# Batch 0's hidden layer by seven products of quarters with sums kept in SBUF, and weight sums and fold in one buffer each

## Chip, cores and metric

The kernel runs on one core of a Trainium2 chip. The metric is device time in microseconds (us), the median of five executions. One further execution was recorded by the hardware profiler; its records are the profile and the trace spoken of below. Engines are named as there: PE (TensorE matmul), PEld (its weight load), DVE (VectorE), ACT (ScalarE), POOL (GpSimd), SP (SyncE, which issues most DMAs).

## What is computed

Four batches of 768 rows pass through attention with hash buckets and then through a Fourier mixing layer with a two-layer channel network:

```python
mask = q_bucket[:, :, :, None] == k_bucket[:, :, None, :]
scores = np.where(mask, scale * (q @ k.T), -1e9)          # (4, 8, 768, 768)
attn = softmax(scores);  x = attn @ v                     # x: (4, 768, 512)
mixed = np.real(fft(fft(x, axis=1), axis=2))
u = x + mixed
un = (u - mean(u)) / sqrt(var(u) + 1e-6)
out = u + np.maximum(un @ w_ch1, 0.0) @ w_ch2             # w_ch1: 512 x 2048, w_ch2: 2048 x 512
```

`w_ch1` and `w_ch2` arrive in 64-bit form, and the kernel narrows them to 32 bits itself. All large products are float32.

## The kernel before

**Stages.** Batch b's attention (`attention`, L912) goes over four pairs of heads, and for each over six tiles of 128 keys, so it has 24 steps. A step computes scores for both heads (`weigh`, L837: PE L856, exponentials on ACT L860, the bucket mask on DVE L866), adds the weights up over key tiles in `acc` (DVE L944) and multiplies the weights of the step before by v (`values`, L872: PE L877). Weights lie in two buffers, `pk`, used in turn. After the sixth tile `scale` (L882) turns the sums into reciprocals (PE L897, DVE L901 to L910) and scales x.

Mixing of batch b (`mix`, L1017) is a generator which is advanced between the attention steps of batch b+1; `MIX`, its number of steps less `LEFT` = 8, is spread over the 24 steps (22 for batch 1). So two streams of work share each engine's queue, and a scheduler fixes the final order of every queue when the kernel is built. `mix` has these parts: `fold` (L984, DVE) forms even and odd parts of x in `ef` and writes `z`; L1034 and L1063 (PE) are the Fourier products, whose results ACT (L1041, L1047) and DVE (L1077) take up; then comes the channel network.

**Hidden layer, two ways.** Batches 1 to 3 use `mlp7` (L1314). It treats `un @ w_ch1` as a product of 2 x 2 quarters and needs seven products where the plain way needs eight. For each of 8 row blocks f, PE computes seven products (L1348: two 128x384 matmuls each) into banks `p1`, `p6`, `p5`, `p7`. They come from a pool of two PSUM buffers; two of the seven accumulate on an earlier product's bank. ACT copies the banks out (L1370, L1373, L1380, L1385, L1389, L1397), DVE adds the copies (L1374, L1381, L1386, L1390, L1398), and ACT applies ReLU (L1377, L1387, L1391, L1399). Three sums of quarters of x (`t1`, `t2`, `t4`, DVE L1334 to L1336, and `t3` in place, L1341) are its right operands. Its left operands, quarters of `w_ch1` and four sums of them, come back from DRAM (`ad`) through a ring of 12 buffers in `w1`'s space.

Batch 0 uses `mlp0` (L1282): eight products per row block straight from `w1` (L1301), and per bank one ReLU on ACT (L1305), nothing on DVE. While it runs, `quarters(f)` (L1129) forms the four sums of row block f on DVE (L1136 to L1139) in `tq` and SP writes them and three plain quarters to `ad` for the later batches; `quarters` for the next f waits until `tq` has been written out.

**Outer layer.** `outer7` (L1194) multiplies half of the hidden rows by `w_ch2`, also by seven products (L1219), so the order in a batch is: first four row blocks, `outer7`, last four row blocks, `outer7`.

**Second weight.** During batch 0's mixing `weights2` (L1161) narrows 16 slices of `w_ch2`. Each is fetched by a DMA on POOL's queue (L677) into one of three raw buffers `zraw2`, then worked on by DVE (L631, L635, L644, and the sums L1185 to L1188) and ACT (L639, L646, L647). The raw buffer is fetched into again when L644 and L647 are through. The first eight slices must be there before the first `outer7`, the last eight can be written only after it and must be there before the second.

**Buffers.** `acc` and `ef` share a pair of buffers, tag `t6`, used in turn.

## Time and profile before

| | |
|---|---|
| Five executions | 1111.12, 1114.02, 1115.25, 1116.39, 1118.21 us; median 1115.25 |
| Profiled execution | 1116.28 us, of which the span of the trace is 1114.5 us |
| PE busy | 1070.0 us, 96% of the span |
| DVE busy | 779.0 us, 70% |
| ACT busy | 453.8 us, 41% |
| POOL busy | 79.7 us, 7% |
| Mean granted PE clock | 0.992 |
| Batch 0's direct products, L1301 | 256 recorded matmuls, from 200.5 us to 381.0 us |
| Seven-product row blocks of batches 1 to 3, L1348 | 672 recorded matmuls |
| Raw slices of `w_ch2`, L677 | 512 KB each, median 4.9 us from issue to landing |

A 32-bit matmul is recorded as two instructions: 128 matmuls of the program are the 256 of L1301. A group's busy time is the time in which at least one of its instructions runs, and[...] a stream of 384-column matmuls of 493 ns each can start every 320 ns or so.

### The profile page before, as it was taken

To read this page: it belongs to the slowest core of one execution; us is meant where nothing else is said; L and a number is where in the kernel's file an instruction comes from. 1 tells how busy PE (TensorE), PEld (TensorE's weight loads), DVE (VectorE), ACT (ScalarE), POOL (GpSimd) and SP (SyncE) were. 2 spreads that over 40 slices of the span, in tenths; PEclk is the share of its full clock that TensorE was granted. 3 is DMA by queue.
4 is the path that set the end of the run, shared out by engine and by line. 5 is a ranking of instruction groups with operands and counts; after the bars stand their busy time and mean duration, and the time that the engine had idled before them with its cause. 6 is when DMAs were issued, how large, how long until landed. Compare 5 with 4: busy or idle time off the path is not lost.

```text
span 1114.5 us, 13886 instructions
## 1 busy us (share of the span) xinstructions
PE 1070.0 (96%) x4917; PEld 654.7 (59%) x4917; DVE 779.0 (70%) x1298; ACT 453.8 (41%) x875; POOL 79.7 (7%) x141
## 2 busy tenths in 40 slices
PE   6989997999999999999999999999999999999996
PEld 3434353555755576655664567645674568768675
DVE  5779977737699595985767796884766875644353
ACT  5767455535054224354325522354315422341420
POOL 0000000001200011030000011021000002100000
PEclk9999999999999999999999999999999999999998
DMA  9743535521037144223144235122032215122401
GB/s 230 191 99 86 109 106 164 156 88 35 1 105 231 42 91 156 43 62 83 32 142 94 72 63 169 26 51 91 24 98 82 71 34 170 46 88 70 139 19 41
DMA packets 175566, 103.13 MB, mean 93 GB/s; under 512 B 129408, under 2 KB 162816, under 8 KB 175488
## 3 DMA queue, kind: packets, MB, share of 16 engines
q1 hardware_dynamic: 168400, 83.93, 28.3%
q0 software_dynamic: 5520, 17.83, 5.1%
q8 instruction: 41, 0.67, 0.2%
q10 hardware_dynamic: 1568, 0.39, 0.2%
q14 instruction: 37, 0.30, 0.1%
HBM read 81.14 MB, written 20.97 MB: 92 GB/s over the span
## 4 chain that ended last, share of the span: by engine, by line
PE 63%; DVE 14%; ACT 2%; issue 2%; DMA 1%; DVEq 0%; ACTq 0%
PE o L1219 23%; PE h_p L1348 18%; PE oo L877 5%; PE h L1301 5%; PE sc L856 5%; DVE pk L866 4%; DVE acc L944 2%; PE cs L1034 2%; PE A L1063 1%; DMA zraw<-in_moe_w_ch_dram 1%; PE B L1063 1%; DVE x L1077 1%; ACT pk L860 1%; PE bits L791 1%; PE sum L897 1%
## 5 line engine op out<-in xcount | busy, mean ns | idle before, releaser
L1219 PE MATMUL o<-w,h 128*128 128x256 f32 x1152 | 258.9, 381 | 0.1
L1219 PEld LDWEIGHTS o<-w,h 128*128 128x128 f32 x1152 | 216.6, 190 | 42.7 <-issue 4.7
L860 ACT ACTIVATE pk<-sc 128x768 f32<-128x768 f32 x192 | 148.2, 808 | 100.9 <-PE sc L856 72.0
L866 DVE SCALAR_TENSOR_TENSOR pk<-qb,kb,pk 128x768 f32<-128x768 bf16 x132 | 128.5, 1012 | 63.3 <-ACT pk L860 62.7
L877 PE MATMUL oo<-pk,vn 128*64 128x385 f32 (+1 forms) x768 | 152.5, 505 | 4.5 <-ACT x L890 3.0
L856 PE MATMUL sc<-qt,kt 64*128 64x384 f32 x768 | 153.7, 505 | 1.9 <-ACT pk L860 1.9
L1348 PE MATMUL h_p<-x,w 128*128 128x384 f32 x384 | 139.0, 493 | 1.4 <-ACT h L1389 1.4
L944 DVE TENSOR_TENSOR acc<-acc,pk 128x1536 f32<-128x1536 f32 (+1 forms) x72 | 105.6, 1480 | 2.4 <-ACT pk L860 1.9
L1348 PE MATMUL h_p<-w 128*128 128x384 f32 x288 | 106.0, 491 | 0.7 <-ACT u L1090 0.7
L877 PEld LDWEIGHTS oo<-pk,vn 128*64 128x64 f32 x768 | 48.9, 137 | 96.0 <-issue 76.1
L1348 PEld LDWEIGHTS h_p<-x,w 128*128 128x128 f32 x384 | 70.4, 190 | 57.7 <-ACT h L1389 5.1
L856 PEld LDWEIGHTS sc<-qt,kt 64*128 64x128 f32 x768 | 66.4, 186 | 48.8 <-issue 24.9
L1301 PE MATMUL h<-x,w 128*128 128x384 f32 x256 | 86.5, 492 | 1.8 <-ACT h L1305 1.8
L1348 PEld LDWEIGHTS h_p<-w 128*128 128x128 f32 x288 | 53.3, 190 | 41.0 <-ACT w L1397 3.3
L1301 PEld LDWEIGHTS h<-x,w 128*128 128x128 f32 x256 | 47.5, 190 | 38.4 <-ACT h L1305 3.0
L1249 ACT COPY tq<-o 128x256 f32<-128x256 f32 x24 | 8.9, 372 | 115.5 <-PE o L1219 115.5
L1231 DVE SCALAR_TENSOR_TENSOR w<-o,rs,w 128x256 f32<-128x256 f32 x56 | 26.7, 478 | 40.7 <-PE o L1219 40.7
L1219 PE MATMUL o<-w 128*128 128x256 f32 x192 | 46.1, 383 | 3.9 <-DVE w L1231 2.4
L972 POOL DMA_DIRECT2D out_dram<-w x30 | 16.3, 546 | 428.3 <-issue 309.0
L1219 PEld LDWEIGHTS o<-w 128*128 128x128 f32 x192 | 35.9, 190 | 11.4 <-DVE w L1231 4.5
L1238 ACT COPY tq<-o 128x256 f32<-128x256 f32 x24 | 8.9, 371 | 74.8 <-PE o L1219 74.8
L1265 DVE TENSOR_TENSOR tq<-tq,o 128x256 f32<-128x256 f32 x24 | 10.1, 421 | 38.1 <-PE o L1219 38.1
(158 smaller groups left out, 1272.8 us busy)
## 6 DMA issues: line engine op xcount, KB each, us to landing
w<-ad SPq DMA_DIRECT2D x168, 128.0 KB, 2.0
w<-bd SPq DMA_DIRECT2D x42, 512.0 KB, 4.5
zraw<-in_moe_w_ch_dram POOLq DMA_DIRECT2D x21, 512.0 KB, 4.9
bd<-w SPq DMA_DIRECT2D x14, 512.0 KB, 5.0
vn<-in_v_dram SPq DMA_DIRECT2D x32, 192.0 KB, 3.5
qn<-in_q_dram SPq DMA_DIRECT2D x120, 48.0 KB, 2.4
kn<-in_k_dram SPq DMA_DIRECT2D x60, 96.0 KB, 3.4
ad<-tq SPq DMA_DIRECT2D x8, 512.0 KB, 3.3
```

What stands on the lines that cost most here:

```text
L856: last[0] = nc.tensor.matmul(ps[:, h, 0:HALF], kt[rows, ks], qt[rows, qs], start=kb is not None, stop=True,)
L860: nc.scalar.activation(pk[:, g, :, 0:HALF], ps[:, :, 0:HALF], AF.Exp, scale=SCALE)
L866: nc.vector.scalar_tensor_tensor(w, qb[:, h].rearrange("p (g s) -> p g s", g=2), kb[:, h, c : c + 1], w, op0=ALU.is_equal, op1=ALU.mult,)
L877: nc.tensor.matmul(oos[g][h * D : (h + 1) * D, 0:w], nat["v", n][:, (2 * c + h) * D : (2 * c + h + 1) * D], pk[:, g, h, 0:w], start=(c == ...
L944: nc.vector.tensor_tensor(acc[:, g], (first if c == 1 else acc)[:, g], new[:, g], op=ALU.add,)
L972: (nc.sync if b == B - 1 else nc.gpsimd).dma_start(out[b, s0 : s0 + 2 * w - 1 : 2, cols], src[at : at + w, cols])
L1034: nc.tensor.matmul(ps[:, pc + 2 * lo : pc + 2 * hi - 1 : 2], z[:, cp, pc, par, t * P : (t + 1) * P], ch[:, cp, pc, lo:hi], start=(cp == 0) ...
L1063: nc.tensor.matmul(ps[:, cols], F[:, par, k, t, j * P : (j + 1) * P], sq[:, t, k, cols], start=(t == 0), stop=(t == 1),)
L1219: nc.tensor.matmul(ps, a[:, r], right7[i][:, r], start=start and r == 0, stop=r == HF // 2 - 1, skip_group_check=not start,)
L1231: nc.vector.scalar_tensor_tensor(t[:, cols], src, r, t[:, cols], op0=ALU.mult, op1=ALU.add)
L1301: nc.tensor.matmul(ps, w1[:, c, fc * P : (fc + 1) * P], x[:, c, cols], start=(c == 0), stop=(c == NDC - 1),)
L1348: nc.tensor.matmul(ps, ring[n % NR][:, k], right[i][:, k], start=start and k == 0, stop=k == 1, skip_group_check=not start,)
```

## The change

`mlp0` is removed and batch 0 uses `mlp7` too, with these differences for `b == 0`. Left operands come from SBUF and not from `ad`: plain quarters straight from `w1`, the four sums straight from `tq`. So `quarters(f + 1)` is called behind the last product of row block f, `quarters(0)` and `quarters(4)` at the start of each half. The ring isn't fetched. `t1` and `t2` lie in a buffer of tag `ef`, `t4` in the third raw buffer of `zraw2`, so `weights2` has two raw buffers left. Both `side` copies share one buffer. The transposes of x for tiles 3 to 5 (`across`) come ahead of the row blocks, those for 0 to 2 behind the fourth. `acc` and `ef` get one buffer each in place of the shared pair, and the fold of batch 1's first half begins one attention step later. Batch 0's mixing has 64 steps where it had 68. Lines behind L1189 have other numbers in the changed kernel: its products are L1338 and its outer products L1218.

```diff
-            acc = wt([P, 2, 2, HALF], F32, "t6", f"acc{n}", 2)
+            acc = wt([P, 2, 2, HALF], F32, "acc", f"acc{n}", 1)
...
-                if c > 2:
+                if c > (3 if b == 1 else 2):
                     next(half, None)
...
-            ef = wt([P, 2, S], F32, "t6", f"ef{b}_{cp}_{pc}", 2)
+            ef = wt([P, 2, S], F32, "ef", f"ef{b}_{cp}_{pc}", 1)
...
-        yield from mlp0(b) if b == 0 else mlp7(b)
+        yield from mlp7(b)
...
-        zt = wt([P, 3, 2 * WC], F32, "z", "zraw2", 1)
-        arrival = Arrival(slices, [zt[:, i] for i in range(3)], NDC * DFF // WC)
+        arrival = Arrival(slices, [zt2[:, i] for i in range(2)], NDC * DFF // WC)
...
+        ut, sd, ss = [*us], side, s1s
+        if b == 0:
+            bt = wt([P, 2, S], F32, "ef", "bt", 1)
+            t1, t2, t4 = (
+                at.rearrange("p (k n) -> p k n", k=2)
+                for at in (bt[:, 0], bt[:, 1], zt2[:, 2, 0:S])
+            )
+            spare = [w1[:, c, 0:DM] for c in range(NDC)]
+            ut = spare[0:3] + [s1s[1].rearrange("p r n -> p (r n)")]
+            sd = [s1s[0].rearrange("p r n -> p (r n)")[:, 0:HALF]] * 2
+            ss = [s1s[0], spare[3].rearrange("p (r n) -> p r n", n=P)]
+            quarters(0)
...
-            if n < len(todo):
+            if b and n < len(todo):
                 nc.sync.dma_start(ring[n % NR], ad[todo[n][0], todo[n][1]])
...
+            left = ring[n % NR]
+            if b == 0:
+                f = n // 7
+                if i >= S2:
+                    left = tq[:, i - S2].rearrange("p (k m) -> p k m", m=P)
+                else:
+                    c, r = (0 if i == A11 else 2), (f + HF if i == A22 else f)
+                    left = w1[:, c : c + 2, r * P : (r + 1) * P]
             for k in range(2):
                 nc.tensor.matmul(
-                    ps, ring[n % NR][:, k], right[i][:, k],
+                    ps, left[:, k], right[i][:, k],
...
+                if b == 0 and r < HF // 2 - 1:
+                    quarters(f + 1)
                 if r % 2:
                     yield
...
+        for half in range(2):
+            if b == 0 and half:
+                quarters(HF // 2)
+            for i, _ in enumerate(inner(half)):
+                if b == 0 and half and i % 4 < 3:
+                    next(arrival2, None)
+                yield
+            if b == 0 and half == 0:
+                for T in range(3):
+                    across(b, T, ut[T])
+            yield from outer7(b, half, hall, ut, rs, ss)
...
-    MIX = [2 + NT + NDC + 2 * (2 * HF + GT * 4)]
-    MIX += [2 + NT + NDC + 2 * (7 * HF // 4 + GT * 4)] * (B - 1)
+    MIX = 2 + NT + NDC + 2 * (7 * HF // 4 + GT * 4)
```

## Prediction

> **What bounds the kernel now.** I read the page first (busy shares, costliest groups), then busy time by stretch around batch 0's mixing, then the timeline of ACT and PE there, then the same stage in batch 1, which runs the new way already.

> ```profile
> span 1114.5 us, 13886 instructions
> ...
> PE 1070.0 (96%) x4917; PEld 654.7 (59%) x4917; DVE 779.0 (70%) x1298; ACT 453.8 (41%) x875; POOL 79.7 (7%) x141
> ...
> L1348 PE MATMUL h_p<-x,w 128*128 128x384 f32 x384 | 139.0, 493 | 1.4 <-ACT h L1389 1.4
> ...
> L1301 PE MATMUL h<-x,w 128*128 128x384 f32 x256 | 86.5, 492 | 1.8 <-ACT h L1305 1.8
> ```

> PE is the bound over the whole, and L1301, the group that is replaced, waits only 1.8 us in all. So PE work removed there is worth its full time only if nothing else gets late. By stretch (columns: span, PE, PEld, DVE, ACT, POOL busy with instructions, clock, DMA):

> ```profile
> 163.80:200.50 36.70, 30.29 (x146) 17.41 (x146) 27.82 (x54) 17.59 (x33) 3.90 (x7) 0.91 0.46 136
> 200.50:254.30 53.80, 52.95 (x190) 27.45 (x188) 28.40 (x44) 21.65 (x42) 2.11 (x4) 1.00 0.44 129
> ...
> 315.90:381.00 65.10, 63.13 (x251) 31.90 (x250) 53.74 (x105) 30.88 (x58) 2.10 (x4) 1.00 0.51 152
> 381.00:431.00 50.00, 49.25 (x239) 37.74 (x238) 38.55 (x72) 12.01 (x25) 8.64 (x17) 1.00 0.48 139
> ```

> Rows 2 and 3 hold the two halves of L1301. In the first half DVE is half idle; in the second it is busy 53.7 of 65.1 us, so there room is short. Row 1, ahead of L1301, is where PE loses most: 6.4 us idle and a clock of 0.91. The timeline says why:

> ```profile
> 184.08 1.58 PE L877 MATMUL oo<-pk,vn 128*64 128x385 f32 x8 [2.80 <-ACT x L890]
> 189.51 1.41 PE L856 MATMUL sc<-qt,kt 64*128 64x384 f32 x4 [1.72 <-ACT pk L860]
> ```

> and on ACT at the same time:

> ```profile
> 188.11 0.67 ACT L639 ACTIVATE zraw<-zraw 128x512 int32<-128x512 uint32 x1 [2.92 <-DMA zraw<-in_moe_w_ch_dram]
> ...
> 196.01 0.68 ACT L639 ACTIVATE zraw<-zraw 128x512 int32<-128x512 uint32 x1 [5.10 <-DMA zraw<-in_moe_w_ch_dram]
> ```

> ACT stands in L639 until a raw slice has landed; what is queued behind (exponentials, L890) is late, and PE with it. Last, a row block of batch 1:

> ```profile
> 498.87 0.56 DVE L1386 TENSOR_TENSOR h<-h,w 128x384 f32<-128x384 f32 x1 [0.79 <-ACT w L1385]
> 499.40 1.45 PE L1348 MATMUL h_p<-w 128*128 128x384 f32 x4
> 499.47 0.52 ACT L1387 ACTIVATE h<-h 128x384 f32<-128x384 f32 x1 [0.62 <-DVE h L1386]
> 499.90 0.46 ACT L1389 COPY h<-h_p 128x384 f32<-128x384 f32 x1
> 500.39 0.56 DVE L1390 TENSOR_TENSOR h<-h 128x384 f32<-128x384 f32 x1 [0.96 <-ACT h L1389]
> 500.41 1.12 PEld L1348 LDWEIGHTS h_p<-x,w 128*128 128x128 f32 x4 [0.17 <-ACT h L1389]
> ```

> The loop to watch: ACT's ReLU L1387 waits for DVE's sum, the copy L1389 stands behind it, and PE's next product waits for the bank which L1389 frees. Here this is just in time.

> [...]

> **PE's gain.** A product of batch 1 (four recorded matmuls) starts 1.29 us behind the one before (494.24, 495.53, 496.82). L1301 runs at the same rate: 48 in 15.75 us. Batch 0 had 256/4 = 64 such groups and gets 224/4 = 56, as the order of the built queues confirms: 8 x 1.29 = 10.3 us less, 5.2 in each half.

> **DVE's and ACT's load.** Start to start, DVE needs 0.47 us for a 384-column sum, 0.335 for a quarter sum (L1136 to L1139), 0.87 for 768 columns, 0.93 for L866, 1.67 for L944. Each half gets 4 x 5 sums of products: 9.4 us. The sums t1 to t4 add 3.5 once. Three of the `quarters` that ran ahead of 200 us now run among the rows of the first half: 3 x 4 x 0.335 = 4.0. First half: 28.4 + 9.4 + 3.5 + 4.0 = 45.3 us of DVE for 53.8 - 5.2 = 48.6 of PE. Second: 53.7 + 9.4, less the fold of batch 1's first half (two times 3.0 us, which moves behind 381 us) = 57.1 for 59.9. ACT has ten operations per row block for four: 24 more of about 0.41 us, 9.8 in each half, to 31.5 and 40.7. No engine is past PE, but 93 to 95% of DVE leaves no room for order.

> **Stretch ahead of the products.** With two raw buffers slice i+2 is fetched when slice i is through. In the built order slice 4's L639 stands directly behind slice 2's L647: a wait of about 5 us; slice 5's about 3. In return L890 moves ahead of slice 2's L639, which takes away the 2.80 us wait, and DVE is rid of three `quarters` with their waits for `tq`. Following the queues by these durations, x is final at 197.7 us for 200.4, and the first product starts at 201.2 with three transposes and a score step done that came later before (3.3 us). That is 203.8 - 201.2 = 2.6 us gained; I take 2.0, since each further wait of ACT counts. Bounds: 6 us gained (all idle time of row 1 gone) and 5 lost (one slice wait more on PE's path).

> **Waits in the rows.** Followed likewise. First half: ACT waits 2.6 us for slice 6 and 1.7 for slice 7, with a copy behind each; PE loses 2.5, less 0.85 that the rows of before lose there. Second half: 0.6 for the sums of block 4 (the left operand now comes straight from DVE), 1.0 behind slice 11, 1.2 for L866 in DVE's queue, 3.3 for slice 14, whose L639 stands behind slice 12's L647 with block 5's copies behind it, 1.4 for ReLUs that wait for DVE: 7.5, less 2.0 of before. Together 10.0 us of waits, 1.25 per row block. `tq` is free again 3.0 us after its last sum (155.15 to 158.16 us); the order leaves 4.2 or more, so I cost that wait at nothing; with SP late it would be up to 1 us per block.

> **Edits with one answer.** `acc` alone: its first sum of a pair waits for PE's L897, which stands ahead of the scores that it needs anyway: nothing (1.5 us per pair if not). `ef` alone: only DVE writes and reads it, in order: nothing, or a gain below 1. `bt` in `ef` and t4 in the raw buffer: read up to block 7, the fold is put behind that. Ring not fetched, `side` shared: nothing. The moved fold puts 6.0 us of DVE into a stretch with 38.55 of 50 busy: 0.7, at most 3. From batch 2's scores on PE's order is nearly unchanged.

> **Sum.** -2.0 ahead, -5.2 + 2.5 - 0.85 = -3.5, -5.2 + 7.5 - 2.0 = +0.3, +0.7 behind: -4.5 us. Against the profiled execution's 1116.3 (span 1114.5 and 1.8 around it) 1111.8; that execution lies 1.0 above the median, so 1110.8.

> **Rivals.** (a) The rows run as in batch 1, where 491.5 to 521.2 us holds 21 products (27.1 us) and 1.4 of other work: 1.2 lost in three blocks, 0.4 each. Then 3.2 us of waits, not 10.0: 1104.0. For: batch 1 has DVE and ACT in the same loop. Against: no slices are narrowed there. (b) Slower: the loop of copy, sum, ReLU and bank sets the pace. If in each block one such sum finds an L944 and an L866 ahead of it, PE waits 1.67 + 0.93 = 2.6 us, in eight blocks 20.8 for 10.0: -4.5 + 10.8 = +6.3, 1121.6. It is a loss from 14.5/8 = 1.8 us per block. For: DVE at 95%, two banks only. Against: in row 3 PE idles 2 us at 83%. (c) Two raw buffers are too few: nothing is gained ahead (2.0) and PE rests long enough for one more 6.8 us at half clock (3.4): 1116.2.

> **How the numbers follow.** Forecast 0.36, (a) 0.27, (b) 0.25, (c) 0.12. 0.5%, 5.6 us, is about what a measurement of this kernel can tell from no change. Faster by more (below 1109.7): 0.11 of the forecast and 0.25 of (a), 0.36. Slower (above 1120.8): 0.01, 0.20 of (b), 0.06 of (c), 0.27. Within: 0.37. The range goes from just below (a) to (b) and 2.4 us of the unknown wait ahead: 1103 to 1124. Cases of both signs share the chance; the forecast's own range is 1107.5 to 1114.

> **What would show it.** Right: 224 matmuls at 1.29 us per product, DVE over 90% busy among the rows, 8 to 12 us of PE waits there with ACT's copies named. Wrong: PE waits under 4 us (a) or over 15 (b) in the rows; a half clock behind slice 4 (c); L897 or SP among the releasers.

## The result, and the profile after

| | Before | After |
|---|---|---|
| Median | 1114.56 us (55 executions, 1110.27 to 1119.22) | 1114.36 us (33 executions, 1111.59 to 1118.29) |
| Profiled execution | 1116.28 us, span 1114.5 | 1114.79 us, span 1113.0 |

The ratio is 0.9996, with a 95% interval of 0.9988 to 1.0005: no difference that can be measured. Batch 0 has eight products fewer, four in each half, and the time stands still. The page of the changed kernel first, its head and the two groups of hidden products that answer to those shown of before:

```profile
span 1113.0 us, 13941 instructions
...
PE 1065.2 (96%) x4885; PEld 648.1 (58%) x4885; DVE 799.8 (72%) x1342; ACT 473.9 (43%) x923; POOL 66.3 (6%) x141
...
L1338 PE MATMUL h_p<-x,w 128*128 128x384 f32 x448 | 163.9, 495 | 3.2 <-ACT h L1379 1.4
...
L1338 PE MATMUL h_p<-w 128*128 128x384 f32 x288 | 106.2, 490 | 0.3
```

32 recorded matmuls fewer on PE (4917 to 4885). Batch 0's products are now part of L1338. By stretch: ahead of the first product, four row blocks, first outer half with the rest of the transposes, last four row blocks, second outer half:

```profile
161.80:199.27 37.47, 32.95 (x168) 18.59 (x165) 30.94 (x56) 21.55 (x40) 3.16 (x6) 0.95 0.48 116
199.27:250.27 51.00, 48.52 (x165) 23.92 (x163) 41.98 (x75) 29.33 (x59) 2.11 (x4) 1.00 0.49 160
250.27:310.25 59.98, 57.47 (x287) 40.01 (x287) 45.19 (x77) 19.23 (x38) 10.16 (x13) 1.00 0.10 21
310.25:375.87 65.62, 61.03 (x235) 29.13 (x234) 58.94 (x114) 42.09 (x85) 2.63 (x5) 0.97 0.55 159
375.87:425.90 50.03, 49.11 (x239) 36.50 (x234) 42.27 (x85) 11.67 (x24) 8.65 (x17) 1.00 0.46 129
```

The fourth row is the one to stop at: 65.6 us, where the old way with 10.3/2 us more of matmuls took 65.1. PE's busy share doesn't show why, since matmuls at half clock count as busy (from 343.7 to 347.1 us PE is busy for 3.40 of 3.40 us, at a clock of 0.50). So I use two measures from the starts of PE's matmuls.

**Shift.** Compare the start of the same matmul in two traces. Before against after: the changed kernel is 1.96 us ahead at 163.4 us, 4.04 at 444.6 us, 1.98 at 1098.6 us. The code up to 163 us is the same, so the first 1.96 are not the change's: they arise between 25 and 35 us, where before waits 0.4 us longer for ACT's L860 and then runs 3.4 us at half clock (from 29.4 us), which costs it some 1.7. The clock records of after have no half clock there. So the change gains 2.08 us up to batch 1's Fourier stage and gives 2.06 back later: nothing is left, as the medians say.

**Loss.** The length of a stretch less what its matmuls take at a steady rate (each kind's usual start-to-start time in the kernel before, 0.3225 us for a 384-column pass of a hidden product). In us, for all kernels of this study; "single buffers" and the other names are those of the experiments below, and "batches 1, 2" runs from batch 1's Fourier stage to batch 3's:

```
                          ahead  first  outer  second outer  batches  half clock in
                                 half   1st    half   2nd    1, 2     161 to 450 us
before                     11.1    6.1    0.8    3.4   -0.6   13.0    6.8
after                       9.3    9.0    1.7    9.0    0.5   15.1    3.4 + 3.4
before, single buffers      9.3    6.1    0.8    5.3   -0.6   15.1    3.4 + 3.4
after, pair of buffers     10.1    9.7    1.7    7.0    0.7   12.8    3.4
after, three raw buffers   10.0    8.3    1.7    8.7    0.5   15.1    3.4
after, pair and three      12.3   13.3    1.7    8.9   -0.5   12.8    6.8 + 6.8
after, even spread         10.1    9.4    1.7    9.1    0.5   15.1    6.8
after, pair and even        9.7    9.2    1.7    9.3    0.7   12.8    3.4
after, no fetches           6.2    7.3    2.2    5.7   -0.1   15.3    0
before, no fetches          5.6    6.2    0.8    2.4   -0.6   12.9    0
after, sums on POOL         9.2    9.6    1.7   16.1   -0.1   15.1    3.4 + 3.4 + 3.4
after, L639 held           10.8    4.2    1.6   10.6    2.7   15.1    3.4 + 3.4 + 3.4
after, held and pair        7.3    5.9    1.6    8.6   -0.2   12.9    0
before, L639 held           9.0    4.8    0.8    3.4   -0.6   12.9    6.8
```

10.3 us of matmuls are gone (32 x 0.3225), and before to after the losses rise by 10.8: -1.8, +2.9, +0.9, +5.6, +1.1, +2.1. That eats the gain, to within the 0.5 us that such a sum can tell. A piece of 3.4 us at half clock is worth some 1.7 us of this (by PE's starts 1.65 at 29.4 us in before and 1.70 at 343.7 us in after), and where it falls differs from one trace to the next.

Two places in the trace of the changed kernel. First the second half, ACT and then PE:

```profile
339.40 0.68 ACT L639 ACTIVATE zraw<-zraw 128x512 int32<-128x512 uint32 x1 [3.08 <-DMA zraw<-in_moe_w_ch_dram]
339.98 1.49 ACT L860 ACTIVATE pk<-sc 128x768 f32<-128x768 f32 x2
341.36 0.84 ACT L729 ACTIVATE sq<-qn 128x768 bf16<-128x768 f32 x1
342.09 0.20 ACT L729 ACTIVATION_READ_ACCUMULATOR sq<-qn 128x1 f32 x1
342.19 0.48 ACT L1363 COPY h<-h_p 128x384 f32<-128x384 f32 x1
```

```profile
342.72 2.04 PE L1338 MATMUL h_p<-bt,tq 128*128 128x384 f32 x4 [2.58 <-ACT h L1363]
344.55 4.00 PE L1338 MATMUL h_p<-x,tq 128*128 128x384 f32 x8
```

The L639 of slice 14 waits 3.08 us for its transfer. Two exponentials and a squaring follow, then the copy L1363, and PE has stood 2.58 us for the bank. The next eight matmuls take 4.00 us where eight take 2.74 at full clock: the clock fell to half at 343.7 us. Second, the boundary between two pairs of heads in batch 1, DVE, before and then after:

```profile
470.40 1.76 DVE L944 TENSOR_TENSOR acc<-pk,pk 128x1536 f32<-128x1536 f32 x1
```

```profile
477.09 0.57 DVE L901 STREAM_TRANSPOSE rt<-sum 128x384 f32<-128x384 f32 x1
477.59 1.71 DVE L944 TENSOR_TENSOR acc<-pk,pk 128x1536 f32<-128x1536 f32 x1
```

The first sum of the new pair (`acc<-pk,pk`) stood early. With one `acc` buffer it is put behind PE's L897 and DVE's first reads of those sums, 7 us later though the changed kernel is 4 us ahead. Who is late is on PE, before and then after:

```profile
484.86 1.51 PE L877 MATMUL oo<-pk,vn 128*64 128x385 f32 x8
```

```profile
483.97 2.35 PE L877 MATMUL oo<-pk,vn 128*64 128x385 f32 x8
```

The eight matmuls of L877 are spread over 0.84 us more. PE's own order changed here too: the next attention step (eight matmuls of L856 and eight of L877) starts at 488.6 us before and at 510.4 after, behind hidden products that it stood ahead of. From 455 us on, PE's order of 2871 recorded matmuls differs between the two kernels at two places alone, this one and the same place in batch 2, and at each of them 1.1 us of shift are lost.

### The profile page after: what moved, and what is told of

Its sections match the earlier page's. It is cut to its first block, busy times and chain, and to the rows that moved or that the text cites. A ratio compares the mean times of both kernels' runs of the same rounds, so it can differ in the third digit from the quotient of the medians.

```text
span 1113.0 us, 13941 instructions
## 1 busy us (share of the span) xinstructions
PE 1065.2 (96%) x4885; PEld 648.1 (58%) x4885; DVE 799.8 (72%) x1342; ACT 473.9 (43%) x923; POOL 66.3 (6%) x141
## 3 DMA queue, kind: packets, MB, share of 16 engines
q1 hardware_dynamic: 168400, 83.93, 28.4%
## 4 chain that ended last, share of the span: by engine, by line
PE 69%; DVE 19%; ACT 4%; DMA 4%; issue 3%; SPq 1%; DVEq 0%; POOL 0%; ACTq 0%
PE h_p L1338 23%; PE o L1218 21%; PE oo L877 7%; PE sc L856 7%; DVE pk L866 3%; DVE acc L944 3%; PE cs L1034 3%; PE sum L897 2%; DMA zraw<-in_moe_w_ch_dram 2%; PE A L1063 2%; ACT pk L860 1%; DMA kn<-in_k_dram 1%; PE B L1063 1%; DVE rt L906 1%; DVE x L910 1%
## 5 line engine op out<-in xcount | busy, mean ns | idle before, releaser
L1218 PE MATMUL o<-w,h 128*128 128x256 f32 x1152 | 259.6, 382 | 1.5 <-ACT w L1090 1.2
L1218 PEld LDWEIGHTS o<-w,h 128*128 128x128 f32 x1152 | 216.3, 190 | 44.0 <-issue 4.0
L860 ACT ACTIVATE pk<-sc 128x768 f32<-128x768 f32 x192 | 148.2, 808 | 98.6 <-PE sc L856 71.4
L1338 PE MATMUL h_p<-x,w 128*128 128x384 f32 x448 | 163.9, 495 | 3.2 <-ACT h L1379 1.4
L866 DVE SCALAR_TENSOR_TENSOR pk<-qb,kb,pk 128x768 f32<-128x768 bf16 x132 | 128.8, 1013 | 44.6 <-ACT pk L860 44.5
L877 PE MATMUL oo<-pk,vn 128*64 128x385 f32 (+1 forms) x768 | 154.1, 500 | 3.4 <-DVE pk L866 3.1
L856 PE MATMUL sc<-qt,kt 64*128 64x384 f32 x768 | 153.2, 502 | 2.2 <-ACT pk L860 2.2
L1338 PEld LDWEIGHTS h_p<-x,w 128*128 128x128 f32 x448 | 81.7, 190 | 70.8 <-ACT h L1379 6.2
L944 DVE TENSOR_TENSOR acc<-acc,pk 128x1536 f32<-128x1536 f32 (+1 forms) x72 | 105.6, 1480 | 8.3 <-ACT pk L860 7.9
L1338 PE MATMUL h_p<-w 128*128 128x384 f32 x288 | 106.2, 490 | 0.3
L877 PEld LDWEIGHTS oo<-pk,vn 128*64 128x64 f32 x768 | 48.8, 136 | 95.6 <-issue 74.5
L856 PEld LDWEIGHTS sc<-qt,kt 64*128 64x128 f32 x768 | 66.3, 186 | 49.8 <-issue 24.4
L1338 PEld LDWEIGHTS h_p<-w 128*128 128x128 f32 x288 | 53.4, 190 | 39.6 <-ACT w L1387 2.5
L1218 PE MATMUL o<-w 128*128 128x256 f32 x176 | 42.2, 383 | 2.9 <-DVE w L1230 2.0
L1364 DVE TENSOR_TENSOR h<-h 128x384 f32<-128x384 f32 x32 | 17.8, 555 | 34.3 <-ACT h L1363 34.3
L1371 DVE TENSOR_TENSOR h<-h 128x384 f32<-128x384 f32 x32 | 17.8, 555 | 31.5 <-ACT h L1370 31.4
L1218 PEld LDWEIGHTS o<-w 128*128 128x128 f32 x176 | 32.9, 190 | 9.6 <-DVE w L1230 4.1
```

The lines of the kernel that those rows point to most:

```text
L856: last[0] = nc.tensor.matmul(ps[:, h, 0:HALF], kt[rows, ks], qt[rows, qs], start=kb is not None, stop=True,)
L860: nc.scalar.activation(pk[:, g, :, 0:HALF], ps[:, :, 0:HALF], AF.Exp, scale=SCALE)
L866: nc.vector.scalar_tensor_tensor(w, qb[:, h].rearrange("p (g s) -> p g s", g=2), kb[:, h, c : c + 1], w, op0=ALU.is_equal, op1=ALU.mult,)
L877: nc.tensor.matmul(oos[g][h * D : (h + 1) * D, 0:w], nat["v", n][:, (2 * c + h) * D : (2 * c + h + 1) * D], pk[:, g, h, 0:w], start=(c == ...
L944: nc.vector.tensor_tensor(acc[:, g], (first if c == 1 else acc)[:, g], new[:, g], op=ALU.add,)
L1218: nc.tensor.matmul(ps, a[:, r], right7[i][:, r], start=start and r == 0, stop=r == HF // 2 - 1, skip_group_check=not start,)
```

## Theories and experiments

Three theories for the missing gain. **Buffers**: the single `acc` costs what the prediction set at nothing. **Slices**: ACT's L639 waits for slices of the second weight, and with copies behind it, no longer ReLUs alone, this takes the gain in the row blocks. **Load**: DVE is too full whatever the slices do. Each experiment was timed together with the kernel before on one chip, where the median of before lay between 1114.08 and 1114.66 us; ratios below are to it.

### One buffer each, alone

```diff
-            acc = wt([P, 2, 2, HALF], F32, "t6", f"acc{n}", 2)
+            acc = wt([P, 2, 2, HALF], F32, "acc", f"acc{n}", 1)
...
-            ef = wt([P, 2, S], F32, "t6", f"ef{b}_{cp}_{pc}", 2)
+            ef = wt([P, 2, S], F32, "ef", f"ef{b}_{cp}_{pc}", 1)
```

> The kernel before with one part of the change alone: `acc` and `ef` in one buffer each. Buffer theory: the first sum of each pair of heads has to wait until PE's L897 has read the old one, DVE then holds the weights longer, exponentials come late, and PE loses about 1.1 us among the rows of batch 1 and 1.1 among those of batch 2: about 2.3 us slower, 1116.9 beside 1114.6. Prediction's step (costs nothing): within 0.5 us, 1114.6.

Measured: 1116.47 us beside 1114.25, ratio 1.0014 [1.0003, 1.0025], near the figure of the buffer theory; the interval alone hardly rules out the 0.5 us of the other, the trace does. The shift against before changes by 0.2 us up to 444 us and by 2.06 behind it, and PE shows the same late L877, in the order of the changed kernel:

```profile
486.38 2.34 PE L877 MATMUL oo<-pk,vn 128*64 128x385 f32 x8
```

The single buffers cost 2.06 us here, where batch 0 has eight products, and 2.28 us in the next experiment, where it has seven. `acc` and `ef` were changed together; that the cost is `acc`'s is read from the order of DVE above and wasn't tested apart.

### The pair again; three raw buffers again; both

```diff
-            acc = wt([P, 2, 2, HALF], F32, "acc", f"acc{n}", 1)
+            acc = wt([P, 2, 2, HALF], F32, "t6", f"acc{n}", 2)
...
-            bt = wt([P, 2, S], F32, "ef", "bt", 1)
+            bt = sq.rearrange("p a b n -> p (a b n)")[:, 0 : 2 * S].rearrange("p (k n) -> p k n", k=2)
```

```diff
-                for at in (bt[:, 0], bt[:, 1], zt2[:, 2, 0:S])
+                for at in (bt[:, 0], bt[:, 1], ch.rearrange("p a b n -> p (a b n)")[:, 0:S])
...
-        arrival = Arrival(slices, [zt2[:, i] for i in range(2)], NDC * DFF // WC)
+        arrival = Arrival(slices, [zt2[:, i] for i in range(3)], NDC * DFF // WC)
```

The first diff is the pair (`ef` and `pwf` likewise, the fold's step as before), the second the raw buffers; the tables that lent their space are fetched again behind the rows.

> The changed kernel with `acc` and `ef` sharing the pair of buffers again (t1 and t2 lie in the space of the cosine table `sq`, which is fetched again behind the rows; the fold of batch 1 is where it was before). Buffer theory: 2.3 us faster than the changed kernel, near 1112.1, with the 1.1 us back in each of batches 1 and 2. If the single buffers cost nothing: 1114.4, and the loss in batches 1 and 2 stays.

> The changed kernel with three raw buffers for the slices of the second weight again (t4 lies in the space of the table `ch`, fetched again behind the rows). Slice theory: ACT's waits for slices in the second half go (the 2.58 us wait of PE at 342.7 us and the half clock behind it, 1.7 us, and about 1 us in the first half), so up to 5 us faster; if two raw buffers are what gained 1.9 us ahead of the rows, some 2 of it is lost there: 1109.5 to 1112. Load theory (DVE too full whatever the slices do): the second half still loses 5 us more than before, within 1 us of 1114.4.

> Both undone together: pair of buffers and three raw buffers, with batch 0's seven products kept. Both theories: the sum of the two runs' gains, about 5 to 7 us faster than the changed kernel, 1107.5 to 1109.5. Load theory alone: not below 1112.

Measured: pair 1115.65 us, 1.0007 [0.9993, 1.0021]; three raw buffers 1113.90, 0.9997 [0.9984, 1.0011]; both 1114.21, 0.9996 [0.9980, 1.0013]. The pair does give 2.28 us back in batches 1 and 2 (shift against the changed kernel), and with it PE's order from there on is exactly that of before; but the median doesn't show it, so that the expectation was missed in the time. The granted clock may be part of why: over the executions of the pair it is 0.9929 in the mean, against 0.9945 for the changed kernel. If the time goes with the clock, 0.0016 of 1114 us is 1.8 us, an estimate. That this lower clock belongs to the pair, and isn't chance, is not shown. With both undone, too, nothing is gained (clock 0.9939 in the mean): by the time alone this run fits "load theory alone, not below 1112".

Three raw buffers gave 0.4 us, not 2 to 5. The reason is in ACT's order there:

```profile
335.19 0.46 ACT L1360 COPY h<-h_p 128x384 f32<-128x384 f32 x1
338.61 0.69 ACT L639 ACTIVATE zraw<-zraw 128x512 int32<-128x512 uint32 x1 [2.96 <-DMA zraw<-in_moe_w_ch_dram]
```

In the built order it is now slice 15 whose L639 stands where slice 14's stood. The scheduler spends the third buffer on running one slice further ahead, and the wait stays (2.96 for 3.08 us). So this run says nothing against the slice theory; it shows only that this buffer didn't cure the order.

### Narrowing spread evenly, alone and with the pair

```diff
-                if b == 0 and half and i % 4 < 3:
+                if b == 0 and half and i % 3 < 2:
```

> The changed kernel with the narrowing of the second weight spread more evenly over the second half (two of three steps in place of three of four): PE's order is the same, and on ACT slice 14's L639 now stands behind block 5's copy L1363. Slice theory (an L639 that waits for its slice, with a copy behind it, is what PE loses most by in the second half): the 2.58 us wait of PE at 342.7 us goes, and the half clock behind it: loss of that stage down from 9.0 us to 4.5 to 6.5, 2.5 to 4.5 us faster than the changed kernel, 1110 to 1112. Load theory (DVE is too full): another wait takes its place, within 1 us of 1114.4.

Measured: 1114.79 us, 0.9999 [0.9990, 1.0008]; the loss among the rows of the second half is 9.1 us for 9.0 in the changed kernel, now without a half clock in it. PE's waits there:

```profile
PE h_p L1338 <- ACT h L1370: 1.7, 1, 1.7
PE h_p L1338 <- DVE tq L1137: 1.3, 1, 1.3
PE h_p L1338 <- ACT w L1387: 1.2, 1, 1.2
PE oo L877 <- DVE pk L866: 0.9, 1, 0.9
PE h_p L1338 <- ACT h L1363: 0.6, 1, 0.6
```

and on ACT what stands ahead of L1387 and of L1370:

```profile
331.85 0.65 ACT L639 ACTIVATE zraw<-zraw 128x512 int32<-128x512 uint32 x1 [2.94 <-DMA zraw<-in_moe_w_ch_dram]
332.41 0.46 ACT L1387 COPY w<-h_p 128x384 f32<-128x384 f32 x1
...
345.29 0.67 ACT L646 ACTIVATE zraw<-zraw 128x512 f32<-128x512 int32 x1 [2.25 <-DVE w L635]
346.13 0.69 ACT L639 ACTIVATE zraw<-zraw 128x512 int32<-128x512 uint32 x1 [0.17 <-DMA zraw<-in_moe_w_ch_dram]
346.71 0.45 ACT L1370 COPY h<-h_p 128x384 f32<-128x384 f32 x1
```

The 2.58 us are gone (0.6 left), and other waits have come, which is what the load theory expected. The 1.2 us in front of L1387 have the chain of the slice theory: transfer, L639, copy, bank, PE. The longest one, 1.7 us in front of L1370, has another: ACT stands 2.25 us in L646 because DVE's L635 is late, and only 0.17 for a transfer. So in this half both theories have waits to show.

The even spread was also run with the pair of buffers:

> The shared pair of buffers for `acc` and `ef` (as in the earlier run) together with the even spread of the narrowing. If both causes stand: 2.1 us of the pair in batches 1 and 2 and 2.5 to 4.5 of the spread, near 1109 in the time and a loss in the second half's rows of 5 us or less. If the spread does nothing: as the run with the pair alone, about 1115.

Measured: 1114.12 us, 0.9999 [0.9989, 1.0009], and 9.3 us lost in the second half's rows. The spread does nothing with the pair either. The pair gives back 2.27 us in batches 1 and 2 here too (shift against the even spread alone).

### No fetches, with the new way and with the old

```diff
                 arrival.fetch(i, nc.gpsimd)
+            arrival.fetch = lambda *_: None
             for i in range(HF):
```

> The changed kernel in which only the first two slices of the second weight are fetched and the other fourteen are narrowed from what lies in the two raw buffers, so the second weight is wrong; all work of the engines stays, no L639 waits for a transfer. Slice theory: PE's waits behind ACT's slice waits go in both halves (about 2 us in the first, 2.6 and the half clock in the second): 4 to 6 us faster, near 1109.5. Load theory: at most 1 us faster; DVE's sums and L944 then hold the copies' banks just as long.

> The kernel before without the fetches of slices 2 to 15 of the second weight (they are narrowed from what lies in the three raw buffers, so the second weight is wrong, and the flag for strange values is taken from the first weight alone). It is what the changed kernel without fetches (first product of batch 1's mixing at 433.65 us) has to be measured against. Slice theory (the slices cost the changed kernel more than the kernel before, since there only ReLUs stand behind them): the first A product of batch 1 comes at 440 to 442 us, 6 to 8 us behind the changed kernel without fetches; in the time 1109 to 1111. If the slices cost both the same: near 436 us, 1106.

The first of them went on, behind its end, to the kernel's second way of computing, which is for strange values; its time (3110 us) says nothing, and its trace is read up to there. By the shift it gains 8.1 us on the changed kernel between 161 and 450 us, more than the 4 to 6 expected. The kernel before without fetches took 1108.69 us, 0.9948 [0.9929, 0.9967], and gains 6.4 us in the same stretch. Neither has a half clock there. My figure for "the slices cost both the same" (436 us) was worked wrong: the changed kernel moved from 442.02 to 433.65, 8.4 us; the same from before's 446.07 is 437.7, and 438.08 was measured.

So the fetches cost both kernels much, by late slices and the half clocks behind them, and the new one only 1.7 us more. (With the fetches their traffic is gone as well, which these runs don't set apart; the run of the kernel before that keeps the fetches and holds L639 back, below, gains 3.9 of the 5.4 us of the median.) They limit both; they are a small part of what ate the gain. Without them the new way gains 3.8 us on the old in this stretch (the shift goes from 0.65 to 4.43), where with them it gained 2.1. What stays lost among the rows, 7.3 and 5.7 us against 6.2 and 2.4, has no slice in it. In the second half of the changed kernel PE waits 1.8 us for DVE's L901, 1.1 for `tq` and 1.0 for a copy; which of DVE's work causes it wasn't tested.

### Four sums of quarters on POOL

```diff
-        nc.vector.tensor_tensor(s1, a21, a22, op=ALU.add)
+        nc.gpsimd.tensor_tensor(s1, a21, a22, op=ALU.add)
```

(the other three likewise)

> The changed kernel with the four sums of w1's quarters (L1136 to L1139) on POOL in place of DVE: DVE has 10.7 us less to do (32 sums at 0.335 us), about 5 of it in each half. Load theory: PE's waits among the rows fall by half, 3 us or more faster, near 1111. Slice theory: only the 1.3 us wait for `tq` can go, and if a sum on POOL takes over 1 us a new wait for `tq` comes in each block: 1113 to 1116.

Measured: 1124.97 us, 1.0093 [1.0077, 1.0109]: 10 us slower, more than any theory gave. A sum takes 1.24 to 1.30 us on POOL for L1136 and L1137, and PE waits 2.4 us for `tq` in the second half. But DVE isn't relieved either. Its groups among the first rows, in the changed kernel:

```profile
L644 DVE CUSTOM_DVE_ANT_0 w<-zraw,w 128x512 uint16<-128x512 uint16 x8 | 3.1, 412 | 0.0
...
L1371 DVE TENSOR_TENSOR h<-h 128x384 f32<-128x384 f32 x4 | 2.2, 553 | 2.0 <-ACT h L1370 2.0
```

and with the sums on POOL:

```profile
L644 DVE CUSTOM_DVE_ANT_0 w<-zraw,w 128x512 uint16<-128x512 uint16 x8 | 4.2, 551 | 0.0
L1371 DVE TENSOR_TENSOR h<-h 128x384 f32<-128x384 f32 x4 | 3.2, 789 | 0.6 <-ACT h L1370 0.6
```

These two take 1.3 to 1.4 times as long, and DVE is busy for 54.2 us among the first rows, against 54.3 in the changed kernel, though the sums are gone. Others keep their time there, as L635 (682 to 685 ns) and L944 (1738 to 1740). It is a matter of meeting: from 203 to 387 us, L1371 takes up to 1.09 us where it overlaps a sum on POOL and at most 0.55 elsewhere, L644 0.94 to 2.03 and at most 0.43. What it is in the meeting that slows them is not shown. So the run doesn't decide on the load theory, as it didn't take the load away.

### L639 held back, alone, with the pair, and in the kernel before

```diff
-        nc.scalar.activation(low, lo.bitcast(U32), AF.Copy, scale=2.0**-29)
+        with tc.issue_after(copied[0].ins) if copied else nullcontext():
+            nc.scalar.activation(low, lo.bitcast(U32), AF.Copy, scale=2.0**-29)
...
-                nc.scalar.copy(c12, p1)
+                copied[:] = [nc.scalar.copy(c12, p1)]
```

(the other five copies likewise; in the kernel before the ReLU L1305)

> The changed kernel with one constraint more on the built order: L639 of a slice is issued behind the last copy of a product that stands ahead of it in the program, so it is not hoisted to within a few instructions of the fetch's release; all else is the same. Slice theory: ACT's waits for slices among the rows go, PE's loss in the two row stages falls from 9.0 and 9.0 us to about 7 and 6, and what the run without fetches gained ahead is in part had too: 3 to 6 us faster than the changed kernel, 1108.5 to 1111.5. If lateness of slices only moves to other places (as in the even spread): 1114.4 within 1 us.

> The held L639 together with the shared pair of buffers for `acc` and `ef`. If both causes stand it has 2 us less than the run with the held L639 alone, all of it in batches 1 and 2: 1106.5 to 1109.5, and faster than both kernels. If neither: 1114.

> The kernel before with the same constraint on L639 (issued behind the last ReLU of batch 0's direct products that stands ahead of it): the control for the run that held L639 and shared the pair, which took 1105.1. If that gain is the slices' alone, and the seven products in batch 0 are worth nothing, this comes to 1105 to 1106 too. If the seven products are worth something once L639 is held, it can't go below the kernel before without fetches (1108.7): 1109 to 1111.5, 4 us or more behind the run with both.

Measured: held alone 1112.11 us, 0.9976 [0.9965, 0.9987]; held with the pair 1105.13, 0.9916 [0.9895, 0.9937]; the kernel before with L639 held 1110.21, 0.9958 [0.9944, 0.9972]. The profile of the first shows none of its gain, as that execution (1116.90) was the slowest of its 22 and has three half clocks in the table's stretches. The second, with six executions, beats both kernels by 9 us. Its stretches (ahead, rows with transposes, first outer half, last rows):

```profile
160.70:199.40 38.70, 36.08 (x186) 20.26 (x184) 35.55 (x57) 21.66 (x40) 2.63 (x5) 1.00 0.44 99
199.40:257.60 58.20, 54.87 (x215) 28.07 (x216) 49.42 (x93) 34.84 (x72) 3.30 (x6) 1.00 0.52 161
257.60:304.40 46.80, 44.88 (x221) 34.26 (x220) 32.08 (x55) 11.35 (x23) 8.88 (x12) 1.00 0.00 1
304.40:369.50 65.10, 59.82 (x235) 28.32 (x233) 61.89 (x117) 43.03 (x87) 3.45 (x6) 1.00 0.56 179
```

The clock is 1.00 in every row. Against the changed kernel it is 6.3 us further ahead by 454 us (some 3.4 of the table's loss there was at half clock) and 2.1 more behind that, the pair's. The control separates the two changes: with L639 held on both sides, the seven products with the pair are 5.1 us better than the eight (1110.21 to 1105.13; by the shift 5.1).

Held alone lies above the time expected, held and pair below it. Among the first four row blocks the slice theory's figure came true with some to spare (4.2 and 5.9 us lost, where about 7 were expected). Among the last four it didn't: 8.6 us are still lost (10.6 for held alone), where 6 were expected, although slices make ACT wait only 1.5 us there. DVE is busy for 61.89 of 65.10 us. The longest of PE's waits there, and what stands ahead of it on ACT and DVE (this kernel is three lines of code longer, so L639 is L642 and L944 is L947):

```profile
336.27 1.75 DVE L947 TENSOR_TENSOR acc<-acc,pk 128x1536 f32<-128x1536 f32 x1
337.94 0.55 DVE L1374 TENSOR_TENSOR h<-h 128x384 f32<-128x384 f32 x1
338.40 0.75 DVE L647 CUSTOM_DVE_ANT_0 w<-zraw,w 128x512 uint16<-128x512 uint16 x2
339.07 0.55 DVE L1379 TENSOR_TENSOR h<-h,w 128x384 f32<-128x384 f32 x1
```

```profile
339.66 0.52 ACT L1380 ACTIVATE h<-h 128x384 f32<-128x384 f32 x1 [3.55 <-DVE h L1379]
340.09 0.46 ACT L1382 COPY h<-h_p 128x384 f32<-128x384 f32 x1
```

```profile
340.60 1.56 PE L1341 MATMUL h_p<-x,w 128*128 128x384 f32 x4 [2.43 <-ACT h L1382]
```

A ReLU waits 3.55 us for DVE's sum L1379, which stands in DVE's queue behind L947 and others without a gap; the copy L1382 stands behind the ReLU, and PE waits 2.43 us for its bank. No wait for a slice is in this chain. It is the load theory's, and the loop that the prediction watched.

## Why the prediction was right and wrong

The forecast was 1110.8, with 1107.5 to 1114 as its own range; 1114.36 lies 3.6 above it, just outside. (It was reckoned from the median of five executions, 1115.25; from the 1114.56 of 55 it would be 1110.1.) The result lies inside the wide range, 1103 to 1124, but that range reaches from rival (a) to rival (b), and most results would have been in it. "No change that can be told" had a chance of 0.37, about as much as faster (0.36). By the steps of the forecast:

- **PE's gain, 8 x 1.29 = 10.3 us**: right. 224 matmuls, 1.29 us from product to product.
- **Ahead of the products, -2.0**: right. Less the 1.96 us that this execution was ahead already, the first product starts at 201.2 us as predicted, with three transposes and a score step done. PE's 2.80 us wait for L890 is gone as foretold. The loss fell by 1.8; before has 6.8 us at half clock in this stretch and after 3.4, and how much of the 1.8 that is was not set apart.
- **Second half, +0.3 (waits +5.5 over before)**: right in size, +5.6 of loss, but in part by luck. The chain for slice 14 is the one foretold (3.3 us predicted, 2.58 measured). The sums of block 4 cost 1.29 for 0.6, and L866 0.7 for 1.2. The waits behind slice 11 (1.0) and for late ReLUs (1.4) aren't among PE's waits. So the waits named come to 4.6 and not 7.5, against 2.0 in before: +2.6. About 1.7 more is the half clock, which the forecast had placed only in rival (c), and the rest is in breaks too short to be listed.
- **First half, -3.5 (waits +2.5 - 0.85)**: too good. The waits among the rows are 2.5 us as foretold, though not where it was foretold: ACT waits 0.04 and 1.04 us for slices 6 and 7 in place of 2.6 and 1.7. PE's waits are 0.7 us behind slice 5's L646, which is late for DVE, 1.1 behind slice 8's L639, which waits 0.32 for its transfer, and 0.7 behind slice 9's (1.55). That they sum to the foretold figure is luck. And the loss up to the second half rose by 3.8 (+2.9 and +0.9) and not by 1.65. What was left out is the outer half: the transposes now stand directly ahead of it, and L1218 waits 1.2 us for their copy (L1090) and 0.45 for DVE (before: 1.1 for DVE). The rest is in breaks below half a us.
- **Fold behind 381 us, +0.7**: 1.1.
- **"`acc` alone ... nothing (1.5 us per pair if not)"**: this step failed. It cost 2.06 us. L897 does stand ahead of the scores on PE; what I missed is that DVE's first sum of the pair then moves behind DVE's own reading of those sums, so that the weight buffers come free late, and an attention step is put 22 us further back in PE's order. It costs where row blocks fill the same stretch, 1.1 us in each of batches 1 and 2, and next to nothing at the other pairs' ends. L897 is not named among the releasers, which I had taken as the sign to look for: the order was changed when the kernel was built, and a view of waits doesn't show an order.
- **"From batch 2's scores on PE's order is nearly unchanged"** was true and no argument: it differs at two places alone, and these are the two at which the 2.06 us are lost.

The misses are 2.1 (first half), 2.1 (`acc`) and 0.5 (second half, fold): 4.7, about the 4.5 us that were forecast as the gain. DVE was to be over 90% busy among the rows: 82% in the first half (41.98 of 51.00), 90% in the second. PE's named waits among all eight row blocks come to 7.1 us, under the 8 to 12 of the forecast and over the 3.2 of rival (a), so this sign met neither. Rival (a), nothing but the waits of batch 1, is out all the same: the loss among the rows rose by 8.5 us. Rival (b) is out as stated, as there is no wait of 2.6 us per block; but one such wait, with an L944 ahead of the sum, is the longest that held and pair still has (2.43 us). Rival (c) is out in its first part, as 1.8 us were gained ahead; in its second a half clock did follow a slice wait, behind slice 14 and not slice 4. (Its 6.8 us are what the trace of before has at half clock from 189.8 us on, behind PE's wait of 1.72 us.)

Open in part: why holding L639 and the pair together give 9 us where the two alone give about 2 and nothing in the medians. Part of it may be clock. The mean granted clock over the executions is 0.9947 for held alone, 0.9929 for the pair alone and 0.9968 for both, and 0.0021 of 1114 us is 2.3 us, again an estimate that takes the time to go with the clock. Of the 7.0 us between held alone and both, it leaves 4.7, of which the pair's 2.1 to 2.3 are known; some 2.5 have no cause that a run shows. Six executions of both lie within 0.9 us; those of held alone spread over 6.6. What sets the last 8.6 us is open too: the longest wait is DVE's, but no run took work off DVE without slowing it.

## What to carry to other kernels

A buffer taken away is priced on the engine that writes it: look for where its first write goes in the built order, and what that engine is late with then. Before an edit is costed on a stage with transfers, take the transfers out of both kernels: a wait that both have doesn't eat the gain, and its cure (here one constraint on the order, worth 4 us in the kernel before and 2 in the changed one) may be worth as much as the edit. A further buffer doesn't cure a wait if the scheduler uses it to run further ahead.
